# A cached-attention decode kernel on one core: the last head's tail moved into a branch, and the idle matmuls cut and moved

## The chip, the cores and the metric

The kernel runs on one core of one Trainium2 chip. Its time is the device time of one execution in microseconds (us); a kernel is quoted by the median of its executions. TensorE is the matmul engine (PE in the profile; PEld is its weight load), DVE the VectorE, ACT the ScalarE, SP the engine that issues the loads.

## The reference, cut to what matters

One token attends over a cache of 65,536 positions, with 8 key/value heads of width 256 and two queries to a head. A small token mixer is added; it costs little and is not argued about here.

```python
B, Sq, D = 1, 1, 448
Hq, Hkv, Sk, Dh = 16, 8, 65536, 256
q = (x @ wq).reshape(B, Sq, Hq, Dh).transpose(0, 2, 1, 3)
k = jnp.repeat(k_cache, 2, axis=1)          # k_cache, v_cache: (1, 8, 65536, 256) bf16
v = jnp.repeat(v_cache, 2, axis=1)
scores = jnp.einsum("bhqd,bhkd->bhqk", q, k) * (Dh ** -0.5)
o = jnp.einsum("bhqk,bhkd->bhqd", softmax(scores), v)
a = o.transpose(0, 2, 1, 3).reshape(B, Sq, Hq * Dh) @ wo
return g * a + (1 - g) * b                  # g: a sigmoid gate; b: the token mixer
```

The two caches are 537 MB, and every byte is used once.

## The kernel before

The cache is cut into 32 blocks of 8 MB of K and 8 MB of V; the code calls a block a pair, `j`, and there are four to a head. For each pair TensorE transposes K (128 tiles), multiplies it by the queries (scores), waits for ScalarE's exponentials, sums them (denominators) and multiplies them by the 128 V tiles. K loads go to a ring; V has one buffer, which is free again when `sem_pv` has been raised for the pair before.

```python
for j in range(NP):                          # SyncE: every large load, in order
    last = j == NP - 1
    if j >= 1:
        eng.wait_ge(sem_tr[NB - 1], BODY * (j - 1) + DC)
    load(kring, A_k_cache, j, 0, HV if last else NV, HV * (j % 2), sem_k)
    if last:
        load(kring, A_k_cache, j, HV, NV, HV, sem_kb)      # last K in two halves
    ...
        eng.wait_ge(sem_pv, j)               # V buffer free
    load(vbuf, A_v_cache, j, 0, NLATE if last else NV, 0, sem_v)
    if last:                                 # last V: 96 tiles, then pieces of 16, 12 and 4
        for (n0, n1), sem in zip(pieces, sem_vp):
            load(vbuf, A_v_cache, j, n0, n1, 0, sem)
```

```python
def spin(n):                                 # idle matmuls; nobody reads the result
    for _ in range(n):
        pe.matmul(kst[:, NB - 1, :], ones_sq[:, :], ktT[:, KTB - 1, 0, 0:512], start=True, stop=True)

def values(j, c0, u16):
    pe.wait_ge(sem_exp, c0 + (BODY + 2))
    for r in range(BODY):
        pe.matmul(acc[:, DENC:SELC], ones_sq[:, :], pT[:, r, :], ...)      # denominators
    ...
    with pe.If(j < NP - 1):
        some(NLATE, NV)                      # V products 96..127
    with pe.Else():
        spin(8)
    some(0, NLATE).then_inc(sem_pv, 1)       # V products 0..95

for g in range(H):                           # a hardware loop, as is the inner one
    for m in range(PPH):                     # j = g * PPH + m
        keys(...)                            # transposes and scores
        values(j, c0, u16)
        ...                                  # mixer part, if j < FT
        with pe.If(j == NP - 2):
            spin(14)
    with pe.If(g < H - 1):
        ...                                  # finish the head
late_values(*pieces[0])                      # the last head's tail, after both loops
pe.wait_ge(s_cp, H)
by_d(sps[:, 0, 0:2 * REP])                   # column products
late_values(pieces[1][0], NV).then_inc(s_late, 1)
pe.wait_ge(sem_wo, 16 * H)
pe.wait_ge(s_oTn, H)
project()
```

The softmax here doesn't subtract the row's maximum and nothing guards it: scores larger than these inputs give would overflow.

Of the kernel before, what the change touches and what calls it, by code (L numbers as in the profile page):

```python
# [12 lines left out]
def bass_gated_mix__gqa_block_cached__mixer_token_mlp__decode_kernel(  # L13
# [17 lines left out]
    H = A_k_cache.shape[1]  # L31
# [4 lines left out]
    REP = HQ // H  # L36
# [14 lines left out]
    NV = BODY * NT  # L51
    NP = NC // BODY
# [11 lines left out]
    NLATE = 96  # L64
    pieces = [(NLATE, 112), (112, 124), (124, NV)]
# [25 lines left out]
    with ctx:  # L91
# [3 lines left out]
        def psum(shape, dt, name):  # L95
            return ctx.enter_context(nc.psum_tensor(name, shape, dt))

        def new_sem(name):
            return ctx.enter_context(nc.semaphore(name))
# [64 lines left out]
        sps = psum([P, 2, 512], f32, "sps")  # L164
# [10 lines left out]
        sem_wo = new_sem("sem_wo")  # L175
# [5 lines left out]
        sem_pv = new_sem("sem_pv")  # L181
# [2 lines left out]
        s_sel = new_sem("s_sel")  # L184
        s_cp = new_sem("s_cp")
        s_late = new_sem("s_late")
        s_d2a = new_sem("s_d2a")
        s_a2d = new_sem("s_a2d")
        s_col = new_sem("s_col")
# [8 lines left out]
        s_oTn = new_sem("s_oTn")  # L198
# [63 lines left out]
        def _(pe):  # L262
# [40 lines left out]
            def keys(c0, *where):  # L303
                transposes(0, c0, *where)
                for k in range(1, BODY):
                    transposes(k, c0 + k, *where)
                    scores(k - 1, c0 + k - 1)
                scores(BODY - 1, c0 + BODY - 1)


            def spin(n):
                for _ in range(n):
                    pe.matmul(kst[:, NB - 1, :], ones_sq[:, :], ktT[:, KTB - 1, 0, 0:512], start=True, stop=True)  # L313


            def values(j, c0, u16):
                pe.wait_ge(sem_exp, c0 + (BODY + 2))
                for r in range(BODY):
                    pe.matmul(acc[:, DENC:SELC], ones_sq[:, :], pT[:, r, :],  # L319
                              start=False, stop=(r == BODY - 1), skip_group_check=True)  # L320

                def some(n0, n1):
                    pe.wait_ge(sem_v, u16)
                    for n in range(n0, n1):
                        r, nt = divmod(n, NT)
                        o = 32 * (n % 4)
                        ins = pe.matmul(acc[o:o + REP, 0:DH], pT[:, r, 2 * nt:2 * nt + 2], vbuf[:, n, :],  # L327
                                        start=False, stop=False, skip_group_check=True)
                    return ins

                with pe.If(j < NP - 1):
                    some(NLATE, NV)
                with pe.Else():
                    spin(8)
                some(0, NLATE).then_inc(sem_pv, 1)

            def piece_wait(n):
                for (n0, _), sem in zip(pieces, sem_vp):
                    if n == n0:
                        pe.wait_ge(sem, 16)  # L340

            def late_values(n0, n1):
                for n in range(n0, n1):
                    r, nt = divmod(n, NT)
                    piece_wait(n)
                    for dj in range(2):
                        ins = pe.matmul(sps[:, 0, dj * REP:(dj + 1) * REP], vbuf[:, n, dj:DH:2],  # L347
                                        pT[:, r, 2 * nt:2 * nt + 2], start=(n == NLATE and dj == 0),
                                        stop=(n == NV - 1), skip_group_check=True)
                return ins  # L350

            def by_d(dst):
                for dj in range(2):
                    ins = pe.matmul(dst[:, dj * REP:(dj + 1) * REP], accs[:, dj:DH:2], sel[:, :],  # L354
                                    start=False, stop=True, skip_group_check=True)
                return ins

            def clear(bank):
                pe.matmul(bank, ones_sq[0:1, :], zrow[0:1, 0:bank.shape[-1]], start=True, stop=True,
                          skip_group_check=True)  # L360

            def project():
                for hh in range(REP):
                    for dj in range(2):
                        j = dj * REP + hh
                        for q in range(NCG):
                            ins = pe.matmul(prj[32 * q:32 * q + 1, 0:WG], oTn[:, j:j + 1],  # L367
                                            wo_sb[:, hh, dj * DM + q * WG:dj * DM + (q + 1) * WG],
                                            start=False, stop=True, skip_group_check=True)
                ins.then_inc(s_proj, 1)  # L370

            pe.sem_inc(sem_qk, 2)
            pe.wait_ge(sem_ident, 1)
# [11 lines left out]
            for dj in range(2):  # L385
                for h in range(HQ):
                    j = dj * HQ + h
# [20 lines left out]
            with nc.Fori(0, H, 1, engines=on, head_slot={pe.engine: 0}) as g:  # L408
                with nc.Fori(0, PPH, 1, engines=on, head_slot={pe.engine: 0}) as m:
                    j = pe.snap(g * PPH + m, min_val=0, max_val=NP - 1)  # L410
                    c0 = pe.snap(j * BODY, min_val=0, max_val=NC)
                    u16 = pe.snap(j * 16 + 16, min_val=16, max_val=16 * NP)
                    keys(c0, j, u16, pe.snap(x2_reg, min_val=0, max_val=NV))
                    values(j, c0, u16)
                    with pe.If(j < FT):
                        pe.wait_ge(s_pb, j + 1)
                        for q in range(NCG):
                            pe.matmul(prj[32 * q:32 * q + 1, WG:2 * WG], w2cur[:, :],
                                      gu[:, q * WG:(q + 1) * WG], start=False, stop=True, skip_group_check=True)
                    pe.reg_sub(x2_reg, NV, x2_reg)  # L420
                    with pe.If(j == NP - 2):
                        spin(14)
                with pe.If(g < H - 1):
                    pe.wait_ge(s_cp, g + 1)
                    clear(acc[:, 0:NACC])
                    by_d(acc[:, SELC:NACC]).then_inc(s_sel, 1)
                    pe.wait_ge(sem_wo, pe.snap(g * 16 + 16, min_val=16, max_val=16 * H))
                    pe.wait_ge(s_oTn, g + 1)
                    project()

            late_values(*pieces[0])
            pe.wait_ge(s_cp, H)
            by_d(sps[:, 0, 0:2 * REP])
            late_values(pieces[1][0], NV).then_inc(s_late, 1)
            pe.wait_ge(sem_wo, 16 * H)
            pe.wait_ge(s_oTn, H)
            project()

        @block.vector
        def _(vec):  # L440
# [84 lines left out]
            def evacuate(k, c):  # L525
                vec.wait_ge(sem_qk, c + 1)
                for b in range(0, NB, 2):
                    vec.wait_ge(sem_tr[b], c + 1)
                    vec.tensor_copy(ktT[:, k % KTB, b, :], kst_b[:, b, :]).then_inc(sem_ev[b], 1)  # L529


            def take(n):
                vec.wait_ge(sem_pv, n)
                vec.tensor_copy(accs[:, :], acc[:, 0:SELC]).then_inc(s_cp, 1)  # L534
                vec.drain()
                vec.reduce_sum(densum[:, :], accs[:, DENC:SELC].rearrange("p (nn hh) -> p hh nn", hh=REP),
                               axis=AX.X)
                vec.drain()
                vec.reciprocal(rden[:, :], densum[:, :])
                vec.drain()  # L540
# [7 lines left out]
            def finish_head(g):  # L548
                take(vec.snap(g * PPH + PPH, min_val=PPH, max_val=NP))
                vec.tensor_copy(qcur[:, :, :], qT[:, :, bass.ds(g * REP + REP, REP)])  # L550
                vec.drain()
                vec.wait_ge(s_sel, g + 1)
                by_head(acc[:, SELC:NACC])
# [11 lines left out]
            with nc.Fori(0, H - 1, 1, engines=on) as g:  # L565
                with nc.Fori(0, PPH, 1, engines=on) as m:
                    j = vec.snap(g * PPH + m, min_val=0, max_val=NP)
# [12 lines left out]
            with nc.Fori(NC - NCPH, NC, BODY, engines=on) as c0:  # L580
                for k in range(BODY):
                    evacuate(k, c0 + k)
            take(NP)
            vec.wait_ge(s_late, 1)
            by_head(sps[:, 0, 0:2 * REP])
            vec.wait_ge(s_proj, H)
# [71 lines left out]
```

## Time and profile before

| | kernel before |
|---|---|
| median of its executions | 1270.92 us (1270.15 to 1271.19) |
| the profiled execution | 1270.05 us, span 1268.1 us |
| last V byte landed | 1262.0 us into the span |
| from there to the end | 6.2 us |

The page's first parts, and its line for the queue of large loads (packets, MB, share of the time of 16 engines):

```profile
PE 912.6 (72%) x17053; PEld 860.7 (68%) x17055; DVE 417.9 (33%) x741; ACT 537.2 (42%) x786; POOL 0.9 (0%) x7
...
DMA  9999999999999999999999999999999999999997
...
q1 hardware_dynamic: 12264, 544.22, 99.4%
```

No compute engine is above 72%, and the loads fill 99.4%. The kernel is a stream of loads with work hung on it. Its length is the time of the stream plus what is left to do after the last byte.

The loads of the last pair, as issues with the time from issue to landing:

```profile
kring<-in_A_k_cache_dram SPq DMA_DIRECT2D x2, 4096.0 KB, 22.8
vbuf<-in_A_v_cache_dram SPq DMA_DIRECT2D x1, 6144.0 KB, 24.4
vbuf<-in_A_v_cache_dram SPq DMA_DIRECT2D x1, 1024.0 KB, 26.5
vbuf<-in_A_v_cache_dram SPq DMA_DIRECT2D x1, 768.0 KB, 27.5
vbuf<-in_A_v_cache_dram SPq DMA_DIRECT2D x1, 256.0 KB, 27.8
```

Taken one by one, the two halves of K were issued at 1214.54 and 1214.91 and took 18.1 and 27.5 us, so they landed at 1232.6 and 1242.4. The large V load was issued at 1232.58 and landed at 1257.0; the last piece was issued at 1234.16 and landed at 1262.0.

Against these landings stands TensorE's timeline (start, duration, line, what, count, and in brackets the idle time before it and its releaser):

```profile
1227.20 5.33 PE L327 MATMUL acc<-vbuf,pT 128*2 128x256 bf16 x128
1232.69 2.97 PE L313 MATMUL kst<-ktT,ones_sq 128*128 128x512 bf16 x13 [0.16 <-issue]
1235.50 3.78 PE L277 MATMUL kst<-ident,kring 128*128 128x128 f32 x32
...
1254.94 1.74 PE L297 MATMUL sps<-qcur,ktT 128*128 128x2 bf16 x64
1257.08 0.37 PE L319 MATMUL acc<-pT,ones_sq 128*128 128x32 bf16 x8 [0.40 <-ACT pT L612]
1257.59 1.67 PE L313 MATMUL kst<-ktT,ones_sq 128*128 128x512 bf16 x7
1259.19 2.79 PE L327 MATMUL acc<-vbuf,pT 128*2 128x256 bf16 x96
1262.72 0.95 PE L347 MATMUL sps<-pT,vbuf 128*128 128x2 bf16 x32 [0.73 <-issue]
1263.53 0.61 PE L354 MATMUL sps<-sel,accs 128*128 128x2 f32 x4
1264.00 0.94 PE L347 MATMUL sps<-pT,vbuf 128*128 128x2 bf16 x32
```

L313 is the idle matmuls. K's first half is there at 1232.6, but the 14 spins hold its transposes until 1235.5. V is there at 1257.0, but its products start at 1259.19, behind 8 more spins. Then 0.73 us pass at the ends of the branch and the two loops. The last V tile is multiplied by 1265.0, 3.0 us after it landed. (A few matmul records are missing: 13 and 7 spins are shown of 14 and 8.)

### The profile page before, as it was taken

To read this page: it belongs to the slowest core of one execution; us is meant where nothing else is said; L and a number is where in the kernel's file an instruction comes from. 1 tells how busy PE (TensorE), PEld (TensorE's weight loads), DVE (VectorE), ACT (ScalarE), POOL (GpSimd) and SP (SyncE) were. 2 spreads that over 40 slices of the span, in tenths; PEclk is the share of its full clock that TensorE was granted. 3 is DMA by queue.
4 is the path that set the end of the run, shared out by engine and by line. 5 is a ranking of instruction groups with operands and counts; after the bars stand their busy time and mean duration, and the time that the engine had idled before them with its cause. 6 is when DMAs were issued, how large, how long until landed. Compare 5 with 4: busy or idle time off the path is not lost.

```text
span 1268.1 us, 38721 instructions
## 1 busy us (share of the span) xinstructions
PE 912.6 (72%) x17053; PEld 860.7 (68%) x17055; DVE 417.9 (33%) x741; ACT 537.2 (42%) x786; POOL 0.9 (0%) x7
## 2 busy tenths in 40 slices
PE   1886668766778666697665876767867678766698
PEld 1776667766678666687665876657866568765687
DVE  2433334333344333343222332223332223331233
ACT  0543345543355433455333553334543245532355
POOL 0000000000000000000000000000000000000000
PEclk9988789788898788888788988789887788887889
DMA  9999999999999999999999999999999999999997
GB/s 411 424 428 438 432 432 428 438 436 430 436 426 438 434 430 440 426 436 432 432 440 426 436 430 436 436 428 434 430 440 432 430 432 430 442 432 430 430 424 323
DMA packets 12366, 544.39 MB, mean 429 GB/s; under 512 B 1345, under 2 KB 3395, under 8 KB 3779
## 3 DMA queue, kind: packets, MB, share of 16 engines
q1 hardware_dynamic: 12264, 544.22, 99.4%
q8 instruction: 8, 0.13, 0.0%
q10 hardware_dynamic: 90, 0.01, 0.0%
q14 instruction: 4, 0.02, 0.0%
HBM read 544.22 MB, written 0.00 MB: 429 GB/s over the span
## 4 chain that ended last, share of the span: by engine, by line
DMA 68%; PE 31%; issue 0%; SPq 0%; DVE 0%; ACT 0%; ACTq 0%
DMA kring<-in_A_k_cache_dram 68%; PE kst L277 25%; PE sps L297 5%; PE acc L327 1%; PE kst L313 0%; PE sps L347 0%; PE acc L319 0%; PE sps L354 0%; ACT pT L612 0%; SPq L217 0%; PE prj L367 0%; SPq L215 0%; DVE out_g L587 0%; DVE oTn L545 0%; ACTq L612 0%
## 5 line engine op out<-in xcount | busy, mean ns | idle before, releaser
L277 PE MATMUL kst<-ident,kring 128*128 128x128 f32 x4096 | 561.5, 298 | 314.7 <-DMA kring<-in_A_k_cache_dram 313.6
L623 ACT ACTIVATE ktT<-kst 128x1024 bf16<-128x1024 bf16 x512 | 499.5, 1021 | 671.2 <-PE kst L277 670.9
L277 PEld LDWEIGHTS kst<-ident,kring 128*128 128x128 f32 x4096 | 511.9, 155 | 324.3 <-issue 321.6
L529 DVE COPY ktT<-kst 128x1024 bf16<-128x1024 bf16 x512 | 354.1, 692 | 775.4 <-PE kst L277 751.9
L297 PEld LDWEIGHTS sps<-qcur,ktT 128*128 128x128 bf16 x8192 | 237.8, 96 | 4.6 <-issue 2.1
L297 PE MATMUL sps<-qcur,ktT 128*128 128x2 bf16 x8192 | 236.6, 163 | 1.9 <-issue 1.9
L327 PE MATMUL acc<-vbuf,pT 128*2 128x256 bf16 x4064 | 142.8, 309 | 3.1 <-issue 3.1
L327 PEld LDWEIGHTS acc<-vbuf,pT 128*2 128x2 bf16 x4064 | 104.8, 94 | 33.1 <-issue 3.9
L612 ACT ACTIVATE pT<-sps 128x32 f32 x256 | 51.8, 202 | 17.0 <-PE sps L297 17.0
L319 PE MATMUL acc<-pT,ones_sq 128*128 128x32 bf16 x256 | 11.7, 178 | 12.7 <-ACT pT L612 12.7
L319 PEld LDWEIGHTS acc<-pT,ones_sq 128*128 128x128 bf16 x256 | 8.6, 97 | 15.4 <-ACT pT L612 15.4
L629 ACT ACTIVATE z_b<-z_b 128x448 bf16<-128x448 bf16 x14 | 8.1, 577 | 20.4 <-DVE z_b L516 20.4
L534 DVE COPY accs<-acc 128x288 f32<-128x288 f32 x8 | 3.7, 458 | 37.9 <-PE acc L327 37.9
L381 PE MATMUL acc<-vbuf 42*128 42x42 bf16 x1 | 0.2, 215 | 8.5 <-DMA b_b<-in_B_b_dram 8.5
L381 PEld LDWEIGHTS acc<-vbuf 42*128 42x128 bf16 x1 | 0.1, 99 | 8.6 <-DMA b_b<-in_B_b_dram 8.6
L510 DVE TENSOR_TENSOR z_b<-wtmp,u_b 128x448 bf16<-128x448 bf16 x14 | 5.5, 393 | 1.0
L522 DVE TENSOR_TENSOR gu<-wtmp,z_b 128x448 bf16<-128x448 bf16 x14 | 5.5, 392 | 1.0
L520 DVE TENSOR_SCALAR z_b<-z_b 128x448 bf16<-128x448 bf16 x14 | 3.9, 277 | 5.9 <-ACT z_b L629 5.9
L508 DVE TENSOR_TENSOR wtmp<-u_b 128x448 bf16<-128x448 bf16 x14 | 5.5, 392 | 1.0
L514 DVE TENSOR_TENSOR z_b<-u_b,wtmp 128x448 bf16<-128x448 bf16 x14 | 5.5, 392 | 1.0
L504 DVE TENSOR_SCALAR wtmp<-hbT,params 128x448 bf16<-128x448 bf16 x14 | 4.7, 337 | 2.6 <-issue 2.6
L506 DVE TENSOR_SCALAR u_b<-wtmp,params 128x448 bf16<-128x448 bf16 x14 | 4.7, 337 | 2.6 <-issue 2.6
(84 smaller groups left out, 80.5 us busy)
## 6 DMA issues: line engine op xcount, KB each, us to landing
kring<-in_A_k_cache_dram SPq DMA_DIRECT2D x2, 4096.0 KB, 22.8
vbuf<-in_A_v_cache_dram SPq DMA_DIRECT2D x1, 6144.0 KB, 24.4
wo_sb<-in_A_wo_dram SPq DMA_DIRECT2D x8, 448.0 KB, 28.6
vbuf<-in_A_wq_dram SPq DMA_DIRECT2D x1, 3072.0 KB, 10.3
vbuf<-in_A_v_cache_dram SPq DMA_DIRECT2D x1, 1024.0 KB, 26.5
vbuf<-in_A_v_cache_dram SPq DMA_DIRECT2D x1, 768.0 KB, 27.5
vbuf<-in_A_wq_dram SPq DMA_DIRECT2D x1, 512.0 KB, 11.1
kring<-in_A_k_cache_dram SPq DMA_DIRECT2D x31, 27.8
```

The costliest lines, as they stand in the source:

```text
L277: ins = pe.transpose(kst[:, b, i * P:(i + 1) * P], kring_f[:, at + NT * (k % DC) + 4 * b + i, :], ident[:, :])
L297: ins = pe.matmul(sps[:, par, 2 * nt:2 * nt + 2], ktT[:, par, b, ntl * DH + dj:(ntl + 1) * DH:2], qcur[:, dj, :], start=(dj == 0), stop=(d ...
L319: pe.matmul(acc[:, DENC:SELC], ones_sq[:, :], pT[:, r, :], start=False, stop=(r == BODY - 1), skip_group_check=True)
L327: ins = pe.matmul(acc[o:o + REP, 0:DH], pT[:, r, 2 * nt:2 * nt + 2], vbuf[:, n, :], start=False, stop=False, skip_group_check=True)
L508: vec.tensor_tensor(W, U, U, op=ALU.mult)
L510: vec.tensor_tensor(Z, W, U, op=ALU.mult)
L514: vec.tensor_tensor(Z, U, W, op=ALU.add)
L522: vec.tensor_tensor(gu[:, :], W, Z, op=ALU.mult).then_inc(s_pb, 1)
L529: vec.tensor_copy(ktT[:, k % KTB, b, :], kst_b[:, b, :]).then_inc(sem_ev[b], 1)
L612: act.activation(pT[:, bass.ds(p0 + k % DC, 1), :].rearrange("p o n -> p (o n)"), sps[:, k % 2, 0:2 * NT], AF.Exp, scale=scale).then_inc(s ...
L623: act.activation(ktT[:, k % KTB, b, :], kst_b[:, b, :], AF.Copy).then_inc(sem_ev[b], 1)
L629: act.activation(z_b[:, :], z_b[:, :], AF.Tanh).then_inc(s_tanh, 1)
```

## The change

The intent: let TensorE spin only in the last pair, only between its scores and its denominators, and reach the tail without leaving the loops. The tail becomes a function called in the else branch, and DVE waits for a semaphore of its own, since `sem_pv` is not raised in the last pair any more. In all other pairs V products 0..95 now come before 96..127.

```diff
+        s_early = new_sem("s_early")
...
             def values(j, c0, u16):
+                with pe.If(j == NP - 1):
+                    spin(8)
                 pe.wait_ge(sem_exp, c0 + (BODY + 2))
...
+                some(0, NLATE).then_inc(s_early, 1)
                 with pe.If(j < NP - 1):
-                    some(NLATE, NV)
+                    some(NLATE, NV).then_inc(sem_pv, 1)
                 with pe.Else():
-                    spin(8)
-                some(0, NLATE).then_inc(sem_pv, 1)
+                    tail()
...
+            def tail():
+                ...                          # the seven lines below, unchanged
...
-                    with pe.If(j == NP - 2):
-                        spin(14)
...
-            late_values(*pieces[0])
-            pe.wait_ge(s_cp, H)
-            by_d(sps[:, 0, 0:2 * REP])
-            late_values(pieces[1][0], NV).then_inc(s_late, 1)
-            pe.wait_ge(sem_wo, 16 * H)
-            pe.wait_ge(s_oTn, H)
-            project()
...
-            take(NP)
+            take(NP, s_early)
```

More of the change, by code (lines that the diff above doesn't have):

```diff
@@ L370, in project @@
                 ins.then_inc(s_proj, 1)
+            def tail():
+                late_values(*pieces[0])
+                pe.wait_ge(s_cp, H)
+                by_d(sps[:, 0, 0:2 * REP])
+                late_values(pieces[1][0], NV).then_inc(s_late, 1)
+                pe.wait_ge(sem_wo, 16 * H)
+                pe.wait_ge(s_oTn, H)
+                project()
             pe.sem_inc(sem_qk, 2)
@@ L529, in evacuate, with take @@
                     vec.tensor_copy(ktT[:, k % KTB, b, :], kst_b[:, b, :]).then_inc(sem_ev[b], 1)
-            def take(n):
-                vec.wait_ge(sem_pv, n)
+            def take(n, sem=sem_pv):
+                vec.wait_ge(sem, n)
                 vec.tensor_copy(accs[:, :], acc[:, 0:SELC]).then_inc(s_cp, 1)
```

## The prediction

The new chain ends at 1262.35 us instead of 1264.97, 2.6 us earlier, which takes the 1270.92 us of before to 1268.3; 1268.4 was predicted. "That grid" is 3.41 us: in the traces of before and after, every half-clock stretch that ends before the span does lasts 3.41 us or two to four times that.

> **What bounds the kernel now.** Part 3 of the page gives the big DMA queue 99.4% of sixteen engines' span, 544 MB; TensorE is busy 72%, and its transposes wait 313.6 us for K (the waits). So the stream of loads sets the time up to its last byte, and only what follows can be gained. The landings in the trace: first half of the last K 1232.6 us, second half 1242.4, the first 96 V tiles 1257.0, the three V pieces 1259.5, 1261.3 and 1261.95. The span ends at 1268.1, 6.15 us after the last V byte.
>
> **Why the tail is 6 us** (timeline and chain of waits). TensorE falls behind the loads in the last pair:
> - The V products of the pair before end at 1232.54, when K has just landed. The 14 spins hold the transposes until 1235.5: 2.9 us lost.
> - Scores end at 1256.7, denominators at 1257.45, 8 spins take 1.67 us, and the early V products start at 1259.26, 2.3 us after their V landed.
> - They end at 1261.98. 0.73 us of "issue" follow (end of the If, two Ifs, two loop ends) before the late V products.
> - Late V products and the head's column products take 2.25 us, to 1264.97; the rest 3.1 us.
>
> **What the change does.** It removes the 14 spins (-2.9 us, all on the chain), moves the 8 spins before the wait for the last exponentials (hides 0.4 us), and puts the tail behind one branch instead of the loop exits (estimate 0.15 us, as other branches here show, instead of 0.73). In every other pair it adds one skipped If, hidden in the 0.4 us wait for the exponentials, and swaps the order of 96 and 32 V products; the V buffer is still freed after all 128. No load is issued later, so the stream should end at the same time.
>
> The loop grows, by the built program, from some 1310 to 1450 TensorE instructions. [...] The trace agrees that the loop stays resident: seven 16 KB fetches by 68 us, then none until 1263. [...] no refetching expected.
>
> **New chain (estimate).** K at 1232.6, transposes at once; scores end near 1253.8; spins to 1255.6; V at 1257.0; 96 products (2.75 us) to 1259.8; branch and first late piece to 1260.8; column products to 1261.3; the last pieces follow their landings, to about 1262.35 instead of 1264.97. Gain about 2.6 us, all on the critical path; more is not to be had, because the last V byte then binds.
>
> **The clock.** [...] the trace's clock records change on that grid. K already waits, so transposes follow V products without a gap; spins plus early products fill the wait for V. I expect full clock until 1262. At half, the 96 products would take about 5.3 us and eat the gain.
>
> **Prediction: 1268.4 us**, 8 in 10 between 1267.4 and 1269.9. Faster by over 2%: 0.5%; within 2%: 98.5%; slower: 1%.
>
> **What would show it.** Right: no spins near 1232; transposes within 0.3 us of K's landing; TensorE idle about 1.2 us before the early V products; under 0.3 us between early and late products; last late product within 0.5 us of the last V landing, itself within 0.5 us of 1262. Wrong: clock 0.5 in the last 35 us; over 0.5 us at the branch[...]; refetches in the loop; a later last landing; transposes waiting over 0.5 us for K's second half.

## The result, and the profile after

| | before | after |
|---|---|---|
| median of six | 1270.95 us | 1267.69 us |
| lowest and highest | 1270.09, 1271.19 | 1267.34, 1268.64 |
| the profiled execution | 1270.05 | 1268.64 |
| last V byte landed | 1262.0 | 1263.1 |
| from there to the end of the span | 6.2 us | 3.7 us |

The ratio is 0.9977 (95% interval 0.9965 to 0.999): within 2%, and clear of 1. Ratios here are the mean time of one kernel's runs over that of the other's of the same rounds, so not quite the ratio of the quoted medians.

The medians are 3.26 us apart. The two profiles are only 1.4 us apart, because before's profiled execution, taken apart from the six, was faster than any of them, while after's was the slowest of its six.

After's last loads, to be set against those of before:

```profile
vbuf<-in_A_v_cache_dram SPq DMA_DIRECT2D x1, 6144.0 KB, 24.3
...
vbuf<-in_A_v_cache_dram SPq DMA_DIRECT2D x1, 256.0 KB, 27.7
```

They were issued at 1233.86 and 1235.43, so V landed at 1258.1 and its last piece at 1263.1. Each is 1.1 us later than before. The first half of K, issued at 1215.82, took 18.0 us and landed at 1233.9, 1.2 us later. TensorE's timeline after:

```profile
1228.48 5.33 PE L330 MATMUL acc<-vbuf,pT 128*2 128x256 bf16 x128
1234.10 3.83 PE L278 MATMUL kst<-ident,kring 128*128 128x128 f32 x32 [0.29 <-DMA kring<-in_A_k_cache_dram]
...
1253.74 1.74 PE L298 MATMUL sps<-qcur,ktT 128*128 128x2 bf16 x64
1255.35 1.89 PE L314 MATMUL kst<-ktT,ones_sq 128*128 128x512 bf16 x8
1257.07 0.35 PE L322 MATMUL acc<-pT,ones_sq 128*128 128x32 bf16 x8
1258.15 2.79 PE L330 MATMUL acc<-vbuf,pT 128*2 128x256 bf16 x96 [0.72 <-DMA vbuf<-in_A_v_cache_dram]
1260.88 0.96 PE L350 MATMUL sps<-pT,vbuf 128*128 128x2 bf16 x32
1261.69 0.61 PE L357 MATMUL sps<-sel,accs 128*128 128x2 f32 x4
1262.51 0.98 PE L350 MATMUL sps<-pT,vbuf 128*128 128x2 bf16 x32 [0.20 <-DMA vbuf<-in_A_v_cache_dram]
```

Transposes, early V products and the last late products are now all released by a DMA. The last late product ends at 1263.49, 0.4 us after its tile landed. There is no gap at all between early and late products. The tail went as predicted. What was not predicted is that the stream itself ended 1.1 us later in this execution.

### The profile page after: what moved, and what is told of

Same layout as the page of the kernel before. It is cut to its first block, busy times and chain, and to the rows that moved or that the text cites. A ratio compares the mean times of both kernels' runs of the same rounds, so it can differ in the third digit from the quotient of the medians.

```text
span 1266.8 us, 38663 instructions
## 1 busy us (share of the span) xinstructions
PE 911.8 (72%) x17041; PEld 862.0 (68%) x17041; DVE 418.1 (33%) x741; ACT 537.4 (42%) x786; POOL 0.9 (0%) x7
## 4 chain that ended last, share of the span: by engine, by line
DMA 68%; PE 30%; issue 1%; SPq 0%; DVE 0%; ACT 0%; ACTq 0%
DMA kring<-in_A_k_cache_dram 66%; PE kst L278 25%; PE sps L298 5%; DMA vbuf<-in_A_v_cache_dram 2%; PE acc L330 1%; PE sps L350 0%; SPq L221 0%; PE acc L322 0%; PE prj L370 0%; ACT pT L615 0%; SPq L218 0%; SPq L216 0%; DVE out_g L590 0%; PE prj L431 0%; DVE oTn L548 0%
## 5 line engine op out<-in xcount | busy, mean ns | idle before, releaser
L330 PEld LDWEIGHTS acc<-vbuf,pT 128*2 128x2 bf16 x4064 | 107.4, 95 | 31.9 <-issue 3.3
```

Source lines behind the costliest of these rows:

```text
L330: ins = pe.matmul(acc[o:o + REP, 0:DH], pT[:, r, 2 * nt:2 * nt + 2], vbuf[:, n, :], start=False, stop=False, skip_group_check=True)
```

## The experiments

Three questions were open.

1. Which part of the change gives the gain?
2. Why did the stream end later in after's profile?
3. Why do executions of both kernels scatter by more than 1 us?

My theory for the first was the 14 spins, with the last V byte as the limit; the rival was the placement of the tail and of the 8 spins. For the other two it was a load stream that runs short near 70 us; the rivals were the clock and the memory.

Every kernel below gave a correct result and was timed in five rounds. A job of four kernels ran on one chip, beside nine executions of the kernel before. The three jobs ran on three chips, and the kernel before had medians of 1271.23, 1270.85 and 1270.90 us in them, so a difference of less than 0.4 us between jobs is not read here. In the paragraphs below, "halves" means that the first K is loaded in two halves, an edit explained in the fourth experiment.

### First job: undo one part, or do one part alone

**Remove the 14 spins alone**, from the kernel before:

```diff
-                    with pe.If(j == NP - 2):
-                        spin(14)
```

> The kernel before without the 14 spins; nothing else changed. My theory (the 14 spins hold the transposes back although K has landed, and once they are gone the last V byte binds): scores end about 2.9 us earlier, denominators and 8 spins are over about 0.7 us before V lands, the 0.7 us at the loop exits fits in before the last piece lands, so this alone reaches the changed kernel: within 0.4 us of 1267.7 us, 3 us under before. Rival (the gain comes from the branch placement and from the moved 8 spins): at most 1 us under before, about 1270.

Measured: 1267.51, 1267.56, 1268.86, 1268.94 and 1269.06 us, ratio 0.998. The median, 1268.86, is not within 0.4 us of 1267.7, so the expectation failed as written. Two of the five are as fast as the changed kernel's best; three are 1.4 us slower. One part of the change reaches the limit, but not in every execution.

**Put the 14 spins back** into the changed kernel:

```diff
                     pe.reg_sub(x2_reg, NV, x2_reg)
+                    with pe.If(j == NP - 2):
+                        spin(14)
```

> The changed kernel with the 14 spins put back at the end of the last pair but one. My theory: K's transposes start 2.9 us late again; 8 spins before the denominators and no loop exits save 0.4 + 0.7 us of the tail, so about 1.1 us under before (1269.8 us) and 1.1 to 2.1 us over the changed kernel. Rival (branch placement makes the gain): as the changed kernel, 1267.7 us.

Measured: 1267.88 to 1269.3, median 1268.21, ratio 0.9979. That is 1.6 us better than I had worked out, and close to the rival. The moves alone are worth nearly as much as the removal alone. The parts do not add; each takes away slack that the other would take away too.

**Remove the 8 spins** from the changed kernel:

```diff
-                with pe.If(j == NP - 1):
-                    spin(8)
```

> The changed kernel without its 8 spins, so none at all. If the spins keep the clock (a 3.4 us stretch with scores and idle time alone is followed by half clock in the traces so far): early V products take about 5.2 us instead of 2.8 and the kernel takes about 2.4 us longer, 1270 us, in most executions. If they are idle ballast: 1267.7 us, and the early V products still take 2.8 us.

Measured: 1268.73 to 1271.08, median 1269.43. That is 1.7 us over the changed kernel, where I had worked out 2.4. In the profiled execution (1269.43 us) the same 96 V products take twice as long:

```profile
1256.98 5.29 PE L328 MATMUL acc<-vbuf,pT 128*2 128x256 bf16 x96 [1.90 <-DMA vbuf<-in_A_v_cache_dram]
```

The windows view gives a granted clock of 0.50 from 1256 to 1262 us in that execution; in the changed kernel's trace, with the spins, it was 1.00 there and the products took 2.79 us. So the 8 spins are not ballast: they keep the clock for the V products. The "traces so far" of the expectation include that of before, where TensorE was busy 1.53 of 3.41 us from 54.02 us, nearly all of it with scores, and the clock was 0.50 over the next 3.41 us.

**Load the first K in two halves**, in the changed kernel. Pair 0 can then start when 4 MB are there, and its V buffer comes free earlier:

```diff
-                load(kring, A_k_cache, j, 0, HV if last else NV, HV * (j % 2), sem_k)
+                if j == 0:
+                    load(kring, A_k_cache, j, HV, NV, 0, sem_k)
+                    load(kring, A_k_cache, j, 0, HV, 0, sem_k0)
+                else:
+                    load(kring, A_k_cache, j, 0, HV if last else NV, HV * (j % 2), sem_k)
...
                 if k == DC:
+                    pe.wait_ge(sem_k0, 16)
```

> The changed kernel with the first K load in two halves, so that TensorE starts pair 0 some 10 us earlier and frees the V buffer earlier. Theory (the two modes of the changed kernel, about 1267.5 and 1268.5, differ by whether the load stream runs dry at 70 us, for about 1.5 us, because the second V load is issued too late): no such hole in the trace, second V load issued near 60 us instead of 70, all executions near 1267.4 us, spread under 0.5 us, median 0.3 us or more under the changed kernel. Rival (the modes come from the end, the clock or the memory): no change of the median, spread 1.3 us as before.

Measured: 1267.37 to 1267.67, median 1267.52, ratio 0.9972. The scatter fell from 1.30 to 0.30 us, as expected; the median fell by only 0.17, not by 0.3. The second V load was issued at 64.0 us, not "near 60", because TensorE still starts pair 0 only at 28.45 us, although the half landed at 22.8; why was not looked into. In its trace the last V byte lands at 1262.1.

### Second job: the two causes of scatter, with the first K in halves throughout

**The kernel before with the first K in halves** (the same edit):

> The kernel before with the first K load in two halves, nothing else. If a dry load stream at 70 us makes the slower mode of the kernel before too: all executions near 1270.0 us, spread under 0.5 us, no hole. With the same edit in both, the change is then worth 2.5 us (1270.0 against 1267.5), which is what my prediction said, and the rest of the measured 3.3 us was the odds of the hole. If the change has a second effect: the difference with the edit in both stays at 3 us or more.

Measured: 1270.40, 1270.64, 1270.64, 1271.52 and 1271.66, median 1270.64, ratio 1.0003. The slower executions stayed. So the short stream does not make the slower mode of the kernel before, and with the edit in both kernels the change is still worth 3.1 us (1270.64 to 1267.52, in two jobs), not 2.5. By the two ratios to the kernel before in the same job, 1.0003 and 0.9972, it would even be 3.9 us. My account of the extra 0.7 us fell.

**Without the 14 spins, first K in halves:**

> The kernel before without the 14 spins, with the first K load in halves. If the removal of the 14 spins alone reaches the limit set by the last V byte: 1267.5 us within 0.2, as the changed kernel with halves; moving the tail and the 8 spins is then worth nothing once the 14 are gone. If the moves are worth something of their own: 0.3 us or more above.

Measured: 1267.27, 1267.45, 1267.75, 1268.89, 1269.05, ratio 0.9978. The median is 0.25 us over 1267.5, where 0.2 was allowed. As in the run that removed the 14 spins without halves, there are fast and slow executions, here three and two, and this time the profiled execution was a slow one (1268.89 us). Its timeline, and its windows (busy time of PE, PEld, DVE, ACT and POOL with counts, then granted clock, DMA share and GB/s):

```profile
1252.74 1.74 PE L303 MATMUL sps<-qcur,ktT 128*128 128x2 bf16 x64
1254.88 0.37 PE L325 MATMUL acc<-pT,ones_sq 128*128 128x32 bf16 x8 [0.40 <-ACT pT L616]
1255.39 2.68 PE L319 MATMUL kst<-ktT,ones_sq 128*128 128x512 bf16 x7
1258.00 3.42 PE L333 MATMUL acc<-vbuf,pT 128*2 128x256 bf16 x96
```

```profile
1252.50:1255.90 3.40, 2.86 (x79) 2.54 (x79) 0.69 (x1) 1.86 (x4) 0.00 (x0) 1.00 0.81 347
1255.90:1259.30 3.40, 3.40 (x34) 1.32 (x36) 0.00 (x0) 0.00 (x0) 0.00 (x0) 0.50 0.97 402
```

At 1255.9 the clock fell to half for 3.4 us. The spins take 2.68 us instead of 1.67 and the V products 3.42 instead of 2.79: 1.6 us in all, close to the 1.5 us between the slow and the fast executions here. The stretch before the fall was mostly scores, the wait for the exponentials, and the denominators; the spins began only 0.5 us before its end.

**The changed kernel with the 14 spins back, first K in halves:**

> The changed kernel with the 14 spins put back and the first K load in halves. From the trace of that kernel without halves (1267.99 us, no hole): 1268.1 us, 0.6 over the changed kernel with halves and 1.9 under the kernel before with halves; the moves alone are then worth nearly as much as the removal alone, and the two overlap instead of adding. My first theory said 1.1 to 2.1 us over.

Measured: 1267.42 to 1268.57, median 1267.77, ratio 0.9977. Moves alone: 2.9 us under before with halves. Removal alone (the run above): 2.9 us by the medians. Both: 3.1. The overlap between the removal and the moves is confirmed. The scatter of this kernel (1.15 us) was not traced to a cause; its profiled execution, 1268.21 us and thus 0.8 us slower than its fastest, had its spins in 1.67 us and its V products in 2.79, as before's trace has them at a granted clock of 1.00, so a clock fall there is not what made that one slow.

**Make the second V load later**, by 14 idle matmuls in pair 0:

```diff
                 with pe.If(j == NP - 1):
                     spin(8)
+                with pe.If(j == 0):
+                    spin(14)
```

> The changed kernel with 14 idle matmuls put into the first pair, ahead of its denominators, so that the first V buffer comes free 3 to 6 us later. If the stream runs dry when the second V load is issued late: a hole of 2 to 6 us near 70 us in the trace, and every execution longer by as much, 1269.5 to 1273 us. If lateness there does not matter: 1267.7 us as the changed kernel.

Measured: 1267.34 to 1268.75, median 1267.58, ratio 0.9976. The experiment missed its aim. The second V load was issued at 69.0 us, earlier than in after's own trace (70.2): the spins ran in time that TensorE otherwise spent waiting in its first pass of the loop, so they delayed nothing (0.56 us of "issue" stood among its first V products, where after's trace has 2.77). Its profiled execution (1268.75 us) did land its last V byte at 1263.2. That is one more point for the theory, but no test.

### Third job: single moves, and a late load that is late

**Without the 14 spins and with the 8 moved; the tail stays after the loops:**

```diff
             def values(j, c0, u16):
+                with pe.If(j == NP - 1):
+                    spin(8)
                 pe.wait_ge(sem_exp, c0 + (BODY + 2))
...
-                with pe.Else():
-                    spin(8)
```

> The kernel before with the first K load in halves, without the 14 spins, and with the 8 spins moved ahead of the wait for the last exponentials; the tail stays after the loops. If the slower executions of the run without the move (1268.9 and 1269.1 us, and half clock in its trace from 1255.9 to 1259.3 us) come from a clock stretch that holds only scores and waiting, the move fills that stretch: all executions within 0.3 us of 1267.5, and the tail's new place is worth nothing. If slower executions stay: near 1269 us in two of five. If the tail's place matters: 0.3 us or more over 1267.5 in all.

Measured: 1267.56 to 1267.89, median 1267.72, ratio 0.9977. Two of the five lie a little more than 0.3 us from 1267.5 (1267.82 and 1267.89), but none is near 1269. The scatter is 0.33 us where it was 1.78 without the move. The trace shows the same scores followed at once by the spins, and V products at full speed, at a granted clock of 1.00 from 1252 to 1262 us:

```profile
1252.80 1.74 PE L303 MATMUL sps<-qcur,ktT 128*128 128x2 bf16 x64
1254.62 1.67 PE L319 MATMUL kst<-ktT,ones_sq 128*128 128x512 bf16 x7
1256.13 0.35 PE L327 MATMUL acc<-pT,ones_sq 128*128 128x32 bf16 x8
1257.21 2.79 PE L335 MATMUL acc<-vbuf,pT 128*2 128x256 bf16 x96 [0.72 <-DMA vbuf<-in_A_v_cache_dram]
```

So the slower executions of this pair of runs go with the clock, and only the place of the spins differs between the two; with five executions of each, two slow against none. The place of the spins is not all there is to scatter, as the run with both moves and the 14 spins kept showed. This kernel has the old tail and is still as fast as the one with the new tail and halves (1267.52 us on another chip job; 0.2 us is not told apart). The tail's new place is worth about nothing once the rest is done.

**Move the 8 spins alone** (14 spins and tail as before, halves):

> The kernel before with the first K load in halves and only the 8 spins moved; 14 spins and tail as before. Worked out from the traces: 0.4 us hidden behind the last exponentials, so about 1270.1 us where the kernel before with halves has 1270.5; and none of its executions at 1271.5, if those are the clock's. If the move gives most of what both moves gave together: near 1268.5 us.

Measured: 1268.92 to 1269.50, median 1269.28, against 1270.64 without the move in another job. The ratio to the kernel before, 0.9989, has an interval to 1.0003 and is not clear of 1. That is 1.4 us by the medians, more than the 0.4 expected and less than the rival's 2.1. No execution was near 1271.5, and the scatter is 0.58 us instead of 1.26. In the two traces, both with spins of 1.67 us and V products of 2.79 as at full clock, scores' start to V products' start fell from 4.25 to 3.62 us: 0.6 us is the move's own, and TensorE reached the scores 0.4 us earlier in this trace. The rest of the 1.4 us is put down to the clock, which these two traces cannot show.

**Move the tail alone** (14 spins, 8 spins after the denominators, halves). From the run with the 14 spins put back and halves, the 8 spins go back behind the denominators:

```diff
-                with pe.If(j == NP - 1):
-                    spin(8)
                 pe.wait_ge(sem_exp, c0 + (BODY + 2))
...
+                with pe.If(j == NP - 1):
+                    spin(8)
                 some(0, NLATE).then_inc(s_early, 1)
```

> The kernel before with the first K load in halves and only the tail moved into the else branch (with its own semaphore, early products first); 14 spins kept, 8 spins after the denominators as before. From the 0.73 us at the loop exits, hidden entirely once the tail is inside: about 1269.8 us where the kernel before with halves has 1270.5, with a slower execution or two about 1 us up if the clock makes them. If the exits cost nothing on the chip: 1270.5.

Measured: 1269.40 to 1270.61, median 1269.68, ratio 0.9993 with an interval to 1.0007. Against before with halves that is 1.0 us, near the 0.73 us of the loop exits. Two slower executions remain, as expected for spins after the denominators; the profiled one (at half clock from 1258.2 to 1261.6) was among them. Together the two moves gave 2.9 us by the medians, more than 1.4 and 1.0; between the two profiled executions it was 2.2. This surplus is not explained.

**Hold the second V load** until pair 1's first K tiles are transposed, in the changed kernel; TensorE's program is untouched:

```diff
                     eng.wait_ge(sem_pv, j)
+                    if j == 1:
+                        eng.wait_ge(sem_tr[NB - 1], BODY + 1)
```

> The changed kernel, its second V load held until the first K tiles of pair 1 are transposed (near 76 us instead of 64 to 70); TensorE's program is untouched. If a late second V load leaves the stream short of work and every lost microsecond is paid at the end: the stream moves clearly less for some 4 to 7 us after 70 us, the last V byte lands that much later than 1262, and every execution takes 1271.5 to 1275 us. If the later landing in the changed kernel's trace had another cause: 1267.7 us.

Measured: 1273.82 to 1275.70, median 1274.06, ratio 1.0026 (interval 1.0013 to 1.0040). Four of the five lie in the expected range; the profiled one is the fifth, 1275.70 us. The issue of the second V load, and the traffic from 70 to 76 us (last column: GB/s), in three kernels. Before:

```profile
68.33 0.33 SPq L220 DMA_DIRECT2D vbuf<-in_A_v_cache_dram  x1
70.00:76.00 6.00, 3.10 (x15) 3.10 (x16) 0.94 (x2) 1.02 (x1) 0.00 (x0) 0.59 0.98 415
```

After:

```profile
70.15 0.33 SPq L221 DMA_DIRECT2D vbuf<-in_A_v_cache_dram  x1
70.00:76.00 6.00, 2.50 (x18) 2.23 (x15) 0.69 (x1) 0.07 (x1) 0.00 (x0) 0.70 0.86 341
```

After, with the second V load held:

```profile
77.97 0.33 SPq L221 DMA_DIRECT2D vbuf<-in_A_v_cache_dram  x1
70.00:76.00 6.00, 2.27 (x24) 1.88 (x14) 0.56 (x1) 0.00 (x0) 0.00 (x0) 0.74 0.05 16
```

The first V of the cache is consumed, and its buffer freed, just as the second K load runs out (it landed at 72.8 us in the traces of before and after). Where the next V load was not issued by then, the DMA engines ran dry (16 GB/s above), and nothing later made it good: in the profiled execution, with the load held to 78.0 us, the last V byte lands at 1270.2 instead of 1262.1 to 1263.1, and by the medians the kernel takes 6.4 us longer than the changed kernel. In all the other traces the last V byte landed at 1261.9 to 1262.4 where that load was issued by 68.4 us (eleven traces), and at 1263.1 to 1263.2 where it was issued at 69.0 or 70.2 (two). The next K load was late in after's trace too (issued at 85.4 us, before at 84.2). But it landed 19.35 us after that V load in both traces, so it only passed on the lateness of the V load.

| kernel | 14 spins | 8 spins | tail | median us | scatter us |
|---|---|---|---|---|---|
| before | kept | after denominators | after loops | 1270.95 | 1.10 |
| before, halves | kept | after denominators | after loops | 1270.64 | 1.26 |
| tail alone, halves | kept | after denominators | in branch | 1269.68 | 1.21 |
| 8 moved alone, halves | kept | before denominators | after loops | 1269.28 | 0.58 |
| both moves, halves | kept | before denominators | in branch | 1267.77 | 1.15 |
| 14 gone alone, halves | gone | after denominators | after loops | 1267.75 | 1.78 |
| 14 gone, 8 moved, halves | gone | before denominators | after loops | 1267.72 | 0.33 |
| after | gone | before denominators | in branch | 1267.69 | 1.30 |
| after, halves | gone | before denominators | in branch | 1267.52 | 0.30 |

The last row is the version I would keep. Its median is level with after's (0.17 us is not told apart here), but none of its five executions took the slower course that two of after's six took.

## Why the prediction was right or wrong

The measured 1267.69 us lies in the range of 1267.4 to 1269.9 us, 0.7 us under the predicted 1268.4. The class (within 2%) was right. That the number came so near is in part luck: the clock falls with the old place of the spins, which make the gain larger, and the late stream in some executions of the changed kernel, which makes it smaller, were both not foreseen and pull in opposite directions.

- **The stream is the limit, and only the tail is to be had: right.** From the last V byte to the end, 6.2 us became 3.7; with halves it is 3.6. Nothing tried went below 1267.27 us in any execution.
- **Transposes at K's landing, early products at V's landing, last late product within 0.5 us: right.** Waits for a DMA of 0.29, 0.72 and 0.20 us now stand before them, and the last late product ended 0.4 us after the last landing. The clock was full from 1232.9 to 1263.6 us, as expected.
- **"TensorE idle about 1.2 us before the early V products": mis-sized.** It was 0.72 or 0.73 us in the trace of after and in those of four variants. The new chain in the prediction runs from the spins straight to V and leaves out the denominators, 0.35 us.
- **"Moves the 8 spins (hides 0.4 us)": mis-sized, and its main effect missed.** The move's own saving is 0.6 us, and it also keeps the clock. With the spins after the denominators, some executions fall into a half-clock stretch in the tail and others do not; two such falls, to 0.50 for 3.4 us, were caught in traces, and the run that has no slow execution differs from one of these two only in the place of the spins. The prediction thought of the clock as a risk of the change, and did not see that kernels with the spins in the old place can pay for it.
- **"Gain about 2.6 us, all on the critical path": right for the fastest executions.** The fastest of six are 1270.09 and 1267.34 us, 2.75 apart. The medians are 3.26 apart. I put the rest down to the clock in most executions of before. That is supported by the run with the 8 moved alone, but no slow execution of the unaltered kernel before was profiled, so for that kernel it is argued, not shown.
- **Estimate of 0.15 us at the branch: it was nothing.** The late products followed the early ones without a gap (no idle time before 1260.88 us in after's timeline). The estimate went by other branches in before's trace, where 0.14 to 0.16 us of "issue" stand at three of them. Of the 0.73 us at the loop exits before the change, 0.28 were left in the two runs that removed only the 14 spins and the If around them, so a large part of it hung on that If and its skipped code; this was not followed up.
- **"The stream should end at the same time": wrong in the profiled execution.** It ended 1.1 us later. The step that failed is the look at the other pairs: I checked that no load waits longer in steady state, and did not check the first pass. There the second V load has hardly any slack: issued at 68.3 us it cost nothing in the trace of before, issued at 69.0 us it was late. Whether the change itself makes that load later is open: after's trace has it at 70.2 us, but four other variants without halves have it anywhere from 65.8 to 69.0.
- **"No refetching expected": right.** In the DMA packets of after's trace eight 16 KB instruction fetches are seen until 77 us and none after. The first pass is another matter, as the last section says.
- **The parts as a sum.** The terms (2.9, 0.4 and 0.6 us) add up to more than the 2.6 us that the last V byte allows, and the prediction cut them there. The runs show the consequence: removal alone and moves alone each give 2.9 us by the medians, both together 3.1.

## What to carry to other kernels

When a stream of loads sets the time, measure from the last landing to the end, and expect fixes before that landing to overlap rather than add up: each is worth only the part of the lateness that the others leave (here 2.9 and 2.9 us alone, 3.1 together). Here the idle matmuls that keep the clock did best straight after the scores, inside a wait that is there anyway; 0.8 us later, behind the denominators, they held up the V products and guarded less (a scatter of 1.78 us against 0.33). And when executions of one kernel scatter by as much as the change is worth, find the modes first: here one was a clock fall in the tail (0.50 for 3.4 us), another a single load issued a microsecond too late at the start (at 69.0 or 70.2 us, where 68.4 was early enough), and one stayed open; and a profile shows one execution only.

## What the traces showed besides

- In the traces of before and after the granted clock was 1.00 or 0.50, and the 45 and 46 half-clock stretches that end before the span does last 3.41, 6.83, 10.24 or 13.65 us. A stretch of 3.4 us ahead of half clock need not be idle: one with TensorE busy 2.86 of 3.40 us by the profile (the run without the 14 spins, halves, from 1252.50 us), mostly with scores of 2 columns, was followed by half clock, and one busy 2.69 of 3.41 us (after, from 1256.82 us, with V products, denominators and the end of the spins) was followed by full clock. What decides it is not settled by these runs. The second case, in the columns used above:

```profile
1256.82:1260.23 3.41, 2.69 (x88) 2.14 (x90) 0.00 (x0) 0.00 (x0) 0.00 (x0) 1.00 0.97 402
1260.23:1263.60 3.37, 3.06 (x96) 2.62 (x84) 0.88 (x4) 0.00 (x0) 0.00 (x0) 1.00 0.30 118
```

- In the kernel before, TensorE did nothing but transposes (of float32 tiles) from 1204.31 to 1207.72 us at a granted clock of 0.50, busy 3.41 of 3.41 us, and the clock was 1.00 over the next stretch:

```profile
1204.31:1207.72 3.41, 3.41 (x18) 3.41 (x17) 1.38 (x2) 1.36 (x2) 0.00 (x0) 0.50 1.06 461
1207.80:1211.10 3.30, 3.30 (x56) 3.29 (x55) 1.76 (x3) 2.63 (x4) 0.00 (x0) 1.00 0.87 377
```

- A loop of about 1450 instructions ran here for 1,190 us without a 16 KB instruction fetch after 77 us. In the first pass, beside a load stream of 378 to 483 GB/s (5 us windows from 45 to 65 us), TensorE stood 1.9 and 3.1 us at two places before the kernel's change and 0.9, 2.6, 2.8, 2.9 and 0.6 us at five after it, all but the last near the fetches (at 53.2 and 60.8 us before; 47.8, 55.6, 63.2, 70.2 and 76.6 after), and not at all there in the second pass. Both places before the change, and the first three after it, lie ahead of the last product with the first V, so they make the second V load later. That the fetches cause it was not tested by a run of its own.
